# Talking-heads attention and a squared-ReLU FFN on one core: spread scores for 30 chunks of the first batch, checked row sums, FFN units in four 64x64 tiles, and a new order of TensorE's units

## The chip, the cores and the metric

The kernel runs on one core of a Trainium2 chip. The metric is the device time of one execution in microseconds (us). Inputs and output lie in HBM as float32; inside the kernel all matmul operands are bf16 and all sums are float32 in PSUM.

## What is computed

There are 8 batches, 12 heads, 448 positions and a head dimension of 64. The scores of the 12 heads are mixed by a 12x12 matrix before the softmax (pre-mixing), the probabilities by another after it (post-mixing). The result, 3584 tokens of 768 features, goes through an FFN of width 2048 with squared ReLU.

```python
scores = scale * np.matmul(q, k.transpose(0, 1, 3, 2))      # 8 x 12 x 448 x 448
scores = np.einsum('bhij,hg->bgij', scores, w_pre)
scores = scores - np.max(scores, axis=-1, keepdims=True)
attn = np.exp(scores)
attn = attn / (np.sum(attn, axis=-1, keepdims=True) + 1e-09)
attn = np.einsum('bhij,hg->bgij', attn, w_post)
attn_out = np.matmul(attn, v)
x = attn_out.transpose(0, 2, 1, 3).reshape(B * S, H * D)    # 3584 x 768
out = np.square(np.maximum(x @ w_in, 0.0)) @ w_out          # 768 -> 2048 -> 768
```

Softmax does not change when a constant is subtracted from all scores of a row. The kernel before uses this and never computes the maximum: it takes exp of the mixed scores as they are.

## The kernel before

**Chunks.** The 448 query positions of a batch are cut into chunks of 10 (`CH`), 45 chunks per batch, the last of 8 handled as two of 4. A chunk of 10 positions by 12 heads fills 120 of 128 partitions: one row per (position, head), 448 keys along the free axis. Chunks go in pairs.

**The usual way of a chunk** (batches 1 to 7, and chunks 22 to 44 of batch 0). `emit_QK` (L891) computes scores of a query tile of 128 positions, two heads at a time (64 rows each, the array in two row tiles) or, for a rest of 64 positions, four at a time in four 64x64 tiles; the result is copied from PSUM to the tile `stage` by ScalarE or VectorE (L460 or L461, in the helper `copy`). A DMA of SyncE's queue (`emit_rel`, L947) then moves a chunk's rows from `stage` into the ring `dring`, so that (position, head) lies on partitions. `emit_pre` (L969) mixes the heads of a pair of chunks with four matmuls in four 64x64 tiles; `after_pre` (L989) takes exp on ScalarE with the row sum beside it (L994), the reciprocal on VectorE (L1008), and multiplies it into the post-mixing weights on GpSimd (L1015). `emit_post` (L1029) does the post-mixing with 16 short matmuls (L1047), whose results are copied to `a2t`.

**The direct way** (chunks 0 to 21 of batch 0). To start without a DMA, VectorE multiplies the transposed queries of batch 0 with the pre-mixing weights (`emit_scale`, L821, 36 instructions at L834), into space that `w_out_sb` and `h2t` do not need yet. `emit_direct` (L846) then gets mixed scores straight from six matmuls of the whole 128x128 array per chunk (L856):

```python
for p in ps_:                                                      # six pairs of heads
    r_ = eng.matmul(ps[:, g.banks[0], 0:S], qs[:, p, y:y + 2, :].rearrange("p i g -> p (i g)"),
                    qkt[:, 0, p, 1, :], start=(p == 0), stop=(...))
```

**AV and FFN.** `emit_AV` (L1090) multiplies a half batch (220 or 228 positions) with V in 64x64 tiles (L1104) and in two column tiles (L1125), and the result is copied to `xt`. `emit_F1` (L1163) is the first FFN layer: a unit gives two of the sixteen 128-blocks of the hidden layer. In batches 0 and 1 (`NFULL = 2`) it uses the whole array (L1173, called "full"), later two row tiles of 64x128 (L1194, "row"). `after_F1` (L1219) does the ReLU on ScalarE or VectorE into one of three buffers `h1t`, and VectorE squares it into `h2t` (L1235). `emit_F2` (L1296) is the second layer, in row tiles (L1316); its result goes to `osb` and by GpSimd's DMAs to the output. The last two tiles use the whole array and SyncE's and ScalarE's queues (`emit_last`, L1256; L1265, L1288).

**What sets the order.** Every piece of work is a task with an engine, a mode of tiling and dependencies. `_Plan` commits the tasks one by one: the other engines' by readiness, TensorE's units in the order of the string `ORDER` (L29), whose digits name ten streams (0 transposes, 1 QK, 2 pre-mixing, 3 post-mixing, 4 AV, 5 direct scores, 6 and 7 first FFN layer, 8 and 9 second). A task marked FLEX goes to ScalarE or VectorE, as the plan's costs have it. Each engine then runs its list in that order, and waits are semaphores. PSUM has eight banks; a unit takes one or two and holds them until they are copied out. A unit whose mode differs from that of the unit before it is a change of tiling; there are 244 in TensorE's list, between modes full (128x128), row (64x128), cols (128x64) and quad (64x64).

At the start TensorE runs some matmuls on constants ("warm", L583) while it waits for the first loads.

Of the kernel before, what the change touches and what calls it, by code (L numbers as in the profile page):

```python
# [23 lines left out]
EVENTS = {"tr": 0.12, "qk": 0.72, "di": 0.2, "po": 0.61, "pr": 1.1, "av": 0.43, "o0": 0.43}  # L24
# [3 lines left out]
INF = float("inf")  # L28
ORDER = (  # L29
    "0001155500055555555555555555513155511155555331555533355551135555552005113555555330023324"  # L30
    "2443310041316261116722326772267633227713367333761142441114223667227631167713226671136713"
    "3277620029333912293921812283383338240024442002661118111833381118132672226773136713376224"
    "2444227761136711166333620027622813822383383337771422444200116667733002277622181183118133"
    "8339122922933912291191139333924244422163613731711631622007227363216372227610016733720208"
    "1383338113822291911393119224244422383138311831384222444223621617311716331620027337226336"
    "2127372001636217337220093191119131922833831181138242444222919313933392242444228318331811"
    "1833622267317216362200733733622167200173622367131720029319131931192228181338113822283833"
    "1842244442444238161336220073373362226761171716337610026733724244412812283382020839111911"
    "3913392291192229319138333811382424442283611673317622673137163167122762226733791229339213"
    "98338242444228338338222868633837226773667733677646444876766776678766776879989999899888"  # L40
# [12 lines left out]
class _Task:  # L53
# [3 lines left out]
                 "done", "bias", "sync", "group", "instrs", "issued", "later", "two")  # L57

    def __init__(self, name, engine, fn, deps, after, cost, prio, sem, seminc, mode, dma,
# [18 lines left out]
        self.sync = ()  # L78
        self.done = self.issued = False
# [9 lines left out]
class _Group:  # L89
# [4 lines left out]
    def __init__(self, n):  # L94
        self.n = n
        self.banks = None
        self.readers = [[] for _ in range(n)]


class _Plan:  # L100
# [44 lines left out]
    def _commit(self, t, e, start):  # L145
# [5 lines left out]
        self.free[e] = start + held  # L151
        t.end = start + lat
# [93 lines left out]
    def _commit_pe(self, t, start):  # L246
        if t.mode != self.mode:
            self.mode = t.mode
        g = t.group
        if g is not None and g.banks is None:  # L250
            _, got = self.find(g.n, self.free[PE])
            g.banks = sorted(got)
            for i, readers in zip(g.banks, g.readers):
# [3 lines left out]
                self.bank_users[i] = readers  # L257
                self.age += 1
                self.bank_age[i] = self.age
# [8 lines left out]
    def next_unit(self, order, at):  # L268
        if at >= len(order):
            return None  # L270
        t = self.streams[int(order[at])][0]
        if t.nwait:
            return None
        est = max(self.free[PE], t.avail)
        if t.group is not None and t.group.banks is None:
            est = max(est, self.find(t.group.n, self.free[PE])[0])
        if t.mode != self.mode:
            est = max(est, self.free[PE] + MODE_SWITCH)
        return (est, t) if est < INF else None

    def run(self, order=""):
        self.start()
        at = 0
        while True:
# [15 lines left out]
            if f is not None and (best is None or f[0] <= best[0]):  # L300
# [3 lines left out]
                self.streams[int(order[at])].pop(0)  # L304
                at += 1
                self._commit_pe(f[1], f[0])
# [12 lines left out]
def bass_talking_heads_attention__then__ffn_squared_relu_kernel(  # L319
# [18 lines left out]
    ND = 22  # L338
    NDW = 16
    DH = 4  # L340
# [23 lines left out]
    with ExitStack() as es:  # L364
# [6 lines left out]
        NDS = 16  # L371
        NPS = 10
# [4 lines left out]
        NFULL = 2  # L377
# [8 lines left out]
        wq = sb("wq", [128, NP, H, H5], DT.bfloat16)  # L386
        wall = sb("wall", [128, NP, 2, H], DT.float32)
        mask2 = sb("mask2", [128, H5], DT.float32)
        wrep2 = sb("wrep2", [128, H], DT.float32)
        wk1 = sb("wk1", [128, 64], DT.bfloat16)  # L390
        wk2b = sb("wk2b", [128, H, H5], DT.bfloat16)
        wk2s = sb("wk2s", [128, NPS, PR], DT.bfloat16)
        rowsum = sb("rowsum", [128, NPS, 1], DT.float32)
# [17 lines left out]
        zrow = sb("zrow", [128, S], DT.bfloat16)  # L411
# [4 lines left out]

        def Sm(name):
            return _Sem(nc.alloc_semaphore(name), name)
# [5 lines left out]
        sem_z = Sm("dz")  # L424
        sem_qk = [[Sm("dqk%d_%d" % (i, x)) for x in range(2)] for i in range(3)]
        sem_v = Sm("dv")
        sem_wq = Sm("dwq")
# [3 lines left out]
        sem_last = Sm("olast")  # L431
        sem_out = [Sm("oslot%d" % i) for i in range(NOS)]

        plan = _Plan(NB)

        def c_pe(t):
            return {PE: (t, t + 190.0)}

        def c_ev(cols):
            return {ACT: (cols / 1.2 + 65.0, cols / 1.2 + 175.0),  # L440
                    DVE: (cols / 0.96 + 72.0, cols / 0.96 + 160.0)}

        def add(name, engine, fn, deps, cost, prio, mode=None, group=None, instrs=0):
            return plan.add(name, engine, fn, deps, cost, prio, "ctr", 1, mode, group=group,
                            instrs=instrs)

        events = {}

        def unit(s, name, fn, deps, ns, mode, group, mms):
            kind = name[:2]  # L450
            was = events.get(kind, 0.0)
            events[kind] = was + EVENTS.get(kind, 0.5)
            n = 2 * mms + int(events[kind]) - int(was)
            t = add(name, PE, fn, deps, c_pe(ns), 0, mode, group, n)
            s.append(t)
            return t

        def copy(eng, en, o, i_):
            if en == ACT:
                return eng.activation(o, i_, AF.Copy)  # L460
# [1050 lines left out]
```

## Time and profile before

| | |
|---|---|
| time, median of 3 runs | 526.3 us (523.89 to 526.61) |
| time of the profiled execution | 521.03 us |
| its span (first to last instruction) | 519.0 us |
| TensorE clock granted | 1.000 |

The profile is one execution. A span row gives an engine's busy time; a slice row has one digit for each of 40 slices of about 13 us, the busy share in tenths. TensorE's matmuls are pipelined, so the duration of one matmul overlaps with the next: what a unit costs is read from the start of one group in the timeline to the start of the next, not from its duration. PE is TensorE's matmuls, PEld its weight loads, DVE VectorE, ACT ScalarE, POOL GpSimd, SP SyncE.

### The profile page before, as it was taken

The page shows a single profiled execution, that of the slowest core. Times are in us where ns is not written, and L with a number is a line of the kernel's source. Part 1 is how long each engine was busy: PE and PEld are TensorE (multiplying, and loading weights), DVE is VectorE, ACT ScalarE, POOL GpSimd, SP SyncE. Part 2 cuts the span into 40 slices and gives each one's busy share as a digit, 9 for nine tenths or more (in the row PEclk, how much of TensorE's full clock was granted, in tenths as well). Part 3 has the DMA queues.
Part 4 walks back from the last instruction along what each step waited for, and adds up shares of the span by engine and source line. Part 5 has one row for each costly group of instructions (what it writes and reads, how often), then busy time and mean ns, then how long its engine had stood idle before and what let it go on. Part 6 is the DMA issues. An engine that isn't in the chain of part 4 may idle for free.

```text
span 519.0 us, 23210 instructions
## 1 busy us (share of the span) xinstructions
PE 505.7 (97%) x9632; PEld 320.0 (62%) x9632; DVE 397.4 (77%) x999; ACT 418.5 (81%) x1206; POOL 204.1 (39%) x404
## 2 busy tenths in 40 slices
PE   7998999999999999999999999999999999999997
PEld 3455767577776564666555665566556565568874
DVE  6966989889889677978897778975897668865430
ACT  3688999889988889898998889988878886887310
POOL 9913445425651455134632357124722332332000
PEclk9999999999999999999999999999999999999999
DMA  8999999746984689647984679537965557632003
GB/s 156 198 217 170 187 192 194 168 109 146 167 177 106 144 162 183 134 87 164 175 163 91 141 165 182 128 72 156 192 103 111 125 131 139 123 87 66 4 23 99
DMA packets 82560, 71.85 MB, mean 138 GB/s; under 512 B 13434, under 2 KB 79946, under 8 KB 82458
## 3 DMA queue, kind: packets, MB, share of 16 engines
q0 software_dynamic: 36944, 32.81, 38.8%
q1 hardware_dynamic: 45226, 37.38, 30.1%
q8 instruction: 77, 1.26, 1.0%
q10 hardware_dynamic: 288, 0.20, 0.1%
q14 instruction: 25, 0.20, 0.1%
HBM read 45.70 MB, written 11.01 MB: 109 GB/s over the span
## 4 chain that ended last, share of the span: by engine, by line
PE 87%; DMA 5%; DVE 4%; ACT 2%; issue 1%; SPq 1%; POOL 0%; POOLq 0%; DVEq 0%
PE ps L1316 26%; PE ps L1194 18%; PE ps L1047 7%; PE ps L977 7%; PE ps L1173 6%; PE ps L1125 6%; PE ps L908 6%; PE ps L856 5%; DMA dring<-stage 3%; PE ps L1265 2%; DVE stage L461 2%; PE ps L759 1%; DMA qraw<-in_q_dram 1%; PE ps L1104 1%; ACT pring L994 1%
## 5 line engine op out<-in xcount | busy, mean ns | idle before, releaser
L994 ACT ACTIVATE pring<-ps 128x448 bf16<-128x448 f32 x360 | 191.1, 555 | 16.3 <-PE ps L977 10.3
L1316 PE MATMUL ps<-w_out_sb,h2t 64*128 64x384 bf16 x1664 | 152.0, 323 | 0.6 <-issue 0.6
L1015 POOL TENSOR_TENSOR wk2s<-wk2b,rinv 128x120 bf16<-128x120 bf16 (+1 forms) x179 | 69.8, 392 | 189.8 <-DVE rinv L1008 188.6
L461 DVE CAST a2t<-ps 128x480 bf16<-128x480 f32 (+1 forms) x192 | 117.3, 640 | 14.7 <-PE ps L1047 13.2
L1194 PE MATMUL ps<-xt,w_in_sb 64*128 64x448 bf16 (+2 forms) x1344 | 121.9, 323 | 0.2
L461 DVE CAST stage<-ps 128x448 bf16<-128x448 f32 (+1 forms) x174 | 104.5, 617 | 15.4 <-PE ps L908 11.5
L460 ACT ACTIVATE stage<-ps 128x448 bf16<-128x448 f32 (+1 forms) x186 | 96.6, 551 | 23.0 <-PE ps L908 21.1
L1316 PEld LDWEIGHTS ps<-w_out_sb,h2t 64*128 64x128 bf16 x1664 | 77.1, 94 | 52.4 <-issue 3.6
L460 ACT ACTIVATE a2t<-ps 128x480 bf16<-128x480 f32 (+1 forms) x176 | 92.8, 574 | 13.6 <-PE ps L1047 13.2
L1194 PEld LDWEIGHTS ps<-xt,w_in_sb 64*128 64x128 bf16 x1344 | 62.2, 94 | 40.4 <-PE ps L977 2.2
L1348 POOL DMA_DIRECT2D out_dram<-osb x59 | 37.1, 634 | 111.3 <-ACT pring L994 42.2
L994 ACT ACTIVATION_READ_ACCUMULATOR pring<-ps 128x1 f32 x360 | 79.0, 219 | 0.0
L1047 PEld LDWEIGHTS ps<-wk2s,pring 60*128 60x128 bf16 x2880 | 56.1, 93 | 21.4 <-issue 3.1
L1047 PE MATMUL ps<-wk2s,pring 60*128 60x60 bf16 x2880 | 61.1, 187 | 1.0 <-issue 0.3
L1226 DVE TENSOR_SCALAR h1t<-ps 128x448 bf16<-128x448 f32 (+2 forms) x102 | 49.0, 488 | 16.5 <-PE ps L1194 14.1
L1008 DVE RECIPROCAL rinv<-rowsum 128x2 f32<-128x2 f32 (+1 forms) x184 | 29.1, 158 | 35.9 <-ACT pring L994 35.0
L977 PE MATMUL ps<-dring,wk 60*64 60x448 bf16 (+1 forms) x676 | 54.5, 362 | 1.5 <-DVE stage L461 0.6
L1235 DVE TENSOR_TENSOR h2t<-h1t 128x448 bf16<-128x448 bf16 (+2 forms) x176 | 52.6, 332 | 0.5 <-ACT h1t L1225 0.2
L908 PE MATMUL ps<-qkt 64*128 64x448 bf16 (+1 forms) x360 | 49.8, 354 | 1.4 <-issue 1.4
L1225 ACT ACTIVATE h1t<-ps 128x448 bf16<-128x448 f32 (+2 forms) x74 | 32.9, 456 | 19.7 <-PE ps L1194 18.0
L1173 PE MATMUL ps<-xt,w_in_sb 128*128 128x220 bf16 (+1 forms) x384 | 41.7, 260 | 0.1
L1173 PEld LDWEIGHTS ps<-xt,w_in_sb 128*128 128x128 bf16 x384 | 34.6, 98 | 5.7 <-DVE h1t L1226 0.9
(59 smaller groups left out, 419.3 us busy)
## 6 DMA issues: line engine op xcount, KB each, us to landing
dring<-stage SPq DMA_DIRECT2D x309, 105.0 KB
out_dram<-osb POOLq DMA_DIRECT2D x45, 192.0 KB, 4.0
qraw<-in_q_dram POOLq DMA_DIRECT2D x42, 112.0 KB, 5.5
kraw<-in_k_dram POOLq DMA_DIRECT2D x42, 112.0 KB, 5.3
w_in_sb<-in_moe_w_in_dram POOLq DMA_DIRECT2D x8, 384.0 KB, 12.7
w_out_sb<-in_moe_w_out_dram POOLq DMA_DIRECT2D x8, 384.0 KB, 8.7
vraw<-in_v_dram POOLq DMA_DIRECT2D x21, 128.0 KB, 5.1
vraw<-in_v_dram POOLq DMA_DIRECT2D x21, 96.0 KB, 5.3
```

Source lines behind the costliest of these rows:

```text
L460: return eng.activation(o, i_, AF.Copy)
L461: return eng.tensor_copy(o, i_)
L908: r_ = eng.matmul(ps[y * w:(y + 1) * w, g.banks[x], 0:S], qkt[r0:r0 + 64, pb, p + y, 0, i0:i0 + w], qkt[r0:r0 + 64, pb, p + y, 1, :], star ...
L977: r_ = eng.matmul(ps[64 * y:64 * y + 64, gr.banks[x], 0:S], wk1[64 * x:64 * x + 64 - R0 * x, :], dring[64 * x:64 * x + 64 - R0 * x, (g0 + ...
L994: return eng.activation(pring[:, pr, 0:S], ps[:, gr.banks[x], 0:S], AF.Exp, accum_out=rowsum[:, pr, :])
L1015: return eng.tensor_tensor(wk2s[:, p0:p0 + n, :], i0.to_broadcast([128, n, PR]), rinv[:, p0:p0 + n, :].to_broadcast([128, n, PR]), ALU.mult)
L1047: r_ = eng.matmul(ps[:, gr.banks[x], o0:o0 + PR], pring[64 * x:64 * x + PR, pr + y, j0:j0 + 2 * PJ], wk2s[64 * x:64 * x + PR, pr + y, :], ...
L1173: r_ = eng.matmul(ps[:, g.banks[0], 0:n], w_in_sb[:, ft, t * 128:(t + 1) * 128], xt[:, ft, c0:c1], start=(ft == 0), stop=(ft == NFT - 1))
L1194: r_ = eng.matmul(ps[:, g.banks[x], 0:n], w_in_sb[64 * y:64 * y + 64, ft, t * 128:(t + 1) * 128], xt[64 * y:64 * y + 64, ft, c0:c1], start ...
L1226: return eng.tensor_scalar(h1t[:, s, 0:n], ps[:, g.banks[x], 0:n], 0.0, None, op0=ALU.max)
L1235: return eng.tensor_tensor(h2t[:, t16, o0:o0 + n], h1t[:, s, 0:n], h1t[:, s, 0:n], ALU.mult)
L1316: r_ = eng.matmul(ps[:, g.banks[hh], 0:FH], h2t[64 * y:64 * y + 64, t16, col:col + 128], w_out_sb[64 * y:64 * y + 64, t16, hh * FH:(hh + 1 ...
```

## The change

Line numbers with "after" are of the changed kernel.

1. **Spread scores.** The direct way goes. For chunks 0 to 29 of batch 0 (`ND` from 22 to 30), `emit_spread` (after L889) copies the queries of each pair of heads unscaled into a zeroed layout `qz` in `h2t`, in 12 copies of 64 partitions x 300 elements (FLEX). `emit_spr` (after L902) computes unmixed scores of a chunk with eight matmuls in four column tiles of 128x32, four at a time; a FLEX copy brings the 128x448 result from PSUM to `dring`; the pre-mixing of these chunks is one matmul of the whole array per chunk, with weights `wkf` that a new small DMA (`wrepf`, four transfers on SyncE's queue) and two VectorE operations prepare. The 36 multiplications, the weights for them, the DMA that zeroed rows of `dring`, and the moves of chunks 22 to 29 through `stage` go. Two fills of 1920 float32 elements per partition (one on VectorE, one on ScalarE) zero `qz` at the start. The loads of `w_out` no longer wait for the direct scores.

```diff
-                    r_ = eng.matmul(ps[:, g.banks[0], 0:S],
-                                    qs[:, p, y:y + 2, :].rearrange("p i g -> p (i g)"),
-                                    qkt[:, 0, p, 1, :],
+                    for n, col, p in todo:
+                        r_ = eng.matmul(ps[32 * col:32 * col + 32, g.banks[0], 0:S],
+                                        qz[:, c, 2 * col + n, :], qkt[:, 0, p, 1, :],
+                                        start=(n == 0), stop=(n == 1))
...
+                def fn_sev(eng, en):
+                    return copy(eng, en, dring[:, c % NDS, :], ps[:, g.banks[0], 0:S])
...
+                    if g0 < ND:
+                        for g in gs:
+                            r_ = eng.matmul(ps[:, gr.banks[g - g0], 0:S],
+                                            wkf[:, :, :].rearrange("p i g -> p (i g)"),
+                                            dring[:, g % NDS, :], start=True, stop=True)
+                        return r_
```

2. **Tiling by unit.** Units of both FFN layers, QK units of 128 positions and pre-mixings can run in one of two or three tilings (`_Flex`, after L107), and the order string says which: a digit is the tiling as before, a letter another one. In quad an FFN unit has four matmuls of 64x64 where the row tiling has two of 64x128. In full, a unit's two halves take one bank each, as they come.

```diff
                         for y in range(2):
                             x = ph ^ y
                             t = t16 + x
+                            for z in range(0, 128, w):
                                 r_ = eng.matmul(
-                                ps[:, g.banks[x], 0:n],
-                                w_in_sb[64 * y:64 * y + 64, ft, t * 128:(t + 1) * 128],
+                                    ps[z:z + w, g.banks[x], 0:n],
+                                    w_in_sb[64 * y:64 * y + 64, ft,
+                                            t * 128 + z:t * 128 + z + w],
                                     xt[64 * y:64 * y + 64, ft, c0:c1],
```

3. **A new order** of TensorE's units (`ORDER`, and with it the lists of all engines). There are 228 changes of tiling in it.

4. **Checked row sums.** All 368 row sums are kept, and after the last exp three VectorE operations test whether each lies between 1e-30 and 1e30; a DMA on SyncE's queue brings the 128 results onto one partition, and VectorE reduces them to one flag. The whole program is built a second time with the row maximum subtracted, and stands in the instruction streams as the taken side of a branch: each engine loads the flag into a register and branches. With sums in range, each engine jumps over this second program to the rest of its list. TensorE branches at its end; ScalarE in front of its last 25 tasks, VectorE of its last 11 (squares), GpSimd and SyncE in front of the last output DMAs.

```diff
+            emit_tasks(eng_name, eng, tasks[:k], fast_waits)
+            eng.wait_ge(t_flag.sem.handle, t_flag.semval)
+            fine = eng.value_load(flag[0:1, 0:1])
+            with eng.If(fine == 0):
+                emit_tasks(eng_name, eng, tasks[k:], fast_waits)
...
+                emit_tasks(eng_name, eng, slow[eng_name], slow_waits)
+            if k < len(tasks):
+                with eng.Else():
+                    emit_tasks(eng_name, eng, tasks[k:], fast_waits)
```

TensorE's list before the branch has 10417 matmuls, against 9632 before. By unit, first layer of the FFN: 62 full, 74 row and 40 quad (before: 64 full, 112 row); second layer: 16 full, 84 row and 12 quad (before: 8 full, 104 row). Of 169 pre-mixings in the usual way, 159 are quad and 10 row (before: 173 quad).

More of the change, by code (lines that the diff above doesn't have):

```diff
@@ L431, in bass_talking_heads_attention__then__ffn_squared_relu_kernel @@
         sem_last = Sm("olast")
+        sem_good = Sm("dgood")
         sem_out = [Sm("oslot%d" % i) for i in range(NOS)]
[L434 to L460, printed above, removed]
-            return eng.tensor_copy(o, i_)
@@ L1455, in emit_engine @@
[L1455 to L1456 removed]
+                               NFT * (n / 2.4 + 4.3), "row", g, 2 * NFT, f,
+                               [("full", NFT * (n / 2.4 + 2.5), NFT),
+                                 ("quad", NFT * (n / 2.4 + QFIX), 4 * NFT)], ph)
+                    t_h.sync = [before] if ph else []
+                    before = t_h
+                f1_done(b, parts, t16, t_h)
+                for x in range(2):
+                    t_r = after_F1(b, parts, t16 + x, t_h, c0, n, g, x)
+                    if x == 0:
+                        f.early.append(t_r)
```

1842 lines of the change are left out of this document (997 added, 845 removed).

## The prediction

> **What bounds the kernel now.** I read the page's busy times and slices first, then the chain.
>
> ```profile
> span 519.0 us, 23210 instructions
> PE 505.7 (97%) x9632; PEld 320.0 (62%) x9632; DVE 397.4 (77%) x999; ACT 418.5 (81%) x1206; POOL 204.1 (39%) x404
> PE   7998999999999999999999999999999999999997
> PE 87%; DMA 5%; DVE 4%; ACT 2%; issue 1%; SPq 1%; POOL 0%; POOLq 0%; DVEq 0%
> q8 instruction: 77, 1.26, 1.0%
> ```
>
> TensorE is busy in every slice and carries 87% of the chain: the kernel gets faster by what TensorE is spared, as long as the others keep up. Whether they do is read by stage (columns: window and its length, then busy us of each engine).
>
> ```profile
> 13.00:52.00 39.00, 36.94 (x623) 20.40 (x617) 29.87 (x84) 30.92 (x89) 17.89 (x32) 1.00 1.14 195
> 52.00:104.00 52.00, 50.84 (x942) 35.59 (x938) 47.17 (x133) 48.33 (x148) 25.46 (x50) 1.00 0.96 185
> 104.00:519.00 415.00, 408.57 (x7904) 258.76 (x7898) 311.54 (x753) 334.72 (x963) 148.94 (x297) 1.00 0.62 127
> ```
>
> From 13 to 52 us (direct scores) VectorE has 9.1 us free and ScalarE 8.1; from 52 to 104 they are 91% and 93% busy, nearly as full as TensorE; later 75% and 81%. So there is a tight place, just behind the part that is rewritten.
>
> A busy PE says nothing of its price per unit. That is read from starts in the timeline:
>
> ```profile
> 250.36 1.30 PE L1194 MATMUL ps<-xt,w_in_sb 64*128 64x448 bf16 x12
> 251.49 0.61 PE L1047 MATMUL ps<-wk2s,pring 60*128 60x60 bf16 x32
> ...
> 252.13 1.30 PE L1194 MATMUL ps<-xt,w_in_sb 64*128 64x448 bf16 x12
> 253.36 0.38 PE L977 MATMUL ps<-dring,wk 64*64 64x448 bf16 x4
> ...
> 254.21 0.38 PE L977 MATMUL ps<-dring,wk 64*64 64x448 bf16 x4
> 254.52 1.31 PE L1194 MATMUL ps<-xt,w_in_sb 64*128 64x448 bf16 x12
> ...
> 261.32 0.36 PE L908 MATMUL ps<-qkt 64*64 64x448 bf16 x4
> 261.51 0.38 PE L977 MATMUL ps<-dring,wk 64*64 64x448 bf16 x4
> ```
>
> An FFN unit followed by another row unit takes 251.49 - 250.36 = 1.13 us, six rounds of 0.189; followed by a quad unit 253.36 - 252.13 = 1.23. A change into quad costs 0.10. Back, a pre-mixing takes 0.31 until the row unit starts (254.52 - 254.21), against 0.19 from quad to quad (261.51 - 261.32): 0.12. I use 0.10 per change of tiling.
>
> **The change, part by part.** First TensorE.
>
> ```profile
> 13.23 7.55 PE L856 MATMUL ps<-qkt,w_out_sb 128*128 128x448 bf16 x39
> 20.71 0.36 PE L908 MATMUL ps<-qkt 64*128 64x448 bf16 x2
> ...
> 47.01 1.32 PE L1125 MATMUL ps<-a2t,vraw 128*64 128x220 bf16 x24
> 48.27 0.62 PE L1047 MATMUL ps<-wk2s,pring 60*128 60x60 bf16 x32
> ```
>
> (20.71 - 13.23 - 0.10) / 39 = 0.189 us per direct matmul. *Direct scores go*: 22 chunks x 6 x 0.189 = -24.9. *Spread scores come*: eight matmuls in four column tiles are two rounds; 24 chunks do them in one unit, 6 chunks in three units of one round, so 24 x 2 + 6 x 3 = 66 rounds. The trace has no 128x32 tile; but its 128x64 tiles (L1125) run two at a time at full rate, 24 in 1.26 - 0.10, so twelve rounds of 0.097 for 220 columns; 66 x 0.189 = +12.5. *Their pre-mixing*: 30 matmuls of the whole array, +5.7. Four pre-mixings in quad (chunks 22 to 29) go, -0.8; ten others take two rounds instead of one, in row tiling, +1.9. One warm matmul less, -0.2. Sum -5.8. *Changes of tiling*: 244 to 228, 16 x 0.10 = -1.6. TensorE together: **-7.4 us**, of which 5.3 fall before the second batch's AV, at 104 us of the old trace (counted with the same prices in both lists).
>
> *FFN units in quad* (40 of 176 first-layer units, 12 second-layer; 40 x 6 + 12 x 8 = 336 rounds): I cost a round like one in row tiling. Before has quad rounds, never 24 in a row; the nearest is two pre-mixings and a transpose:
>
> ```profile
> 195.81 0.57 PE L977 MATMUL ps<-dring,wk 64*64 64x448 bf16 x8
> 196.21 0.39 PE L759 MATMUL ps<-ident,qraw 64*64 64x64 bf16 x28
> 196.43 0.43 PE L759 MATMUL ps<-ident,kraw 64*64 64x64 bf16 x28
> ```
>
> Two rounds in 0.40: 0.02 above 2 x 0.19, once per entry, and contained in the price of a change. A transpose puts 28 loads and 28 matmuls into 0.22 us, so neither issue nor loading limits four tiles. I take 0; if every round paid what the first does (0.024: the 0.40 are 0.213 and 0.189, read finer), it would be +8.1. Nothing excludes a gain, but no row suggests one.
>
> *ScalarE and VectorE*, in the first 50 us:
>
> ```profile
> L834 DVE TENSOR_TENSOR w_out_sb<-qkt,wq 128x480 bf16<-128x480 bf16 x24 | 9.6, 445 | 0.1
> L834 DVE TENSOR_TENSOR h2t<-qkt,wq 128x480 bf16<-128x480 bf16 x6 | 2.6, 444 | 0.0
> L834 DVE TENSOR_TENSOR h2t<-qkt,wq 128x240 bf16<-128x240 bf16 x6 | 1.5, 293 | 0.0
> L547 DVE TENSOR_SCALAR wq<-wall 64x180 bf16<-64x180 f32 x4 | 1.2, 330 | 0.6 <-DMA wall<-in_w_pre_dram 0.6
> L816 ACT ACTIVATE w_out_sb<-wk 128x768 bf16<-128x768 bf16 x1 | 0.8, 842 | 0.0
> L460 ACT ACTIVATE stage<-ps 128x448 bf16<-128x448 f32 x149 | 76.9, 555 | 19.4 <-PE ps L908 18.0 <-issue 1.1
> L461 DVE CAST stage<-ps 128x448 bf16<-128x448 f32 x127 | 75.7, 615 | 11.1 <-PE ps L908 10.0 <-PE ps L1047 0.3
> L461 DVE COPY qkt<-ps 128x448 bf16<-128x448 bf16 x11 | 3.9, 380 | 0.7 <-PE ps L755 0.7
> L519 DVE MEMSET zrow<- 4x224 uint32 x1 | 0.2, 245 | 0.1
> ```
>
> Gone: 13.7 us of multiplications, 1.2 of weights, about 1.2 of fills. Added: 30 copies from PSUM, half on each engine, 15 x 0.555 + 15 x 0.615 = 17.6; twelve query copies of 300 elements, about 0.3 each, 3.6; two zero fills of 1920 elements (224 take 0.245, 768 on ScalarE 0.84), about 2.0 each, 4.0. Net +9 of busy time for the two. The fills fall into the wait for the first loads, so some 5 remain. At 13 to 52 us there were 9.1 + 8.1 = 17.2 free; less 5, and less 5.3 on each engine because TensorE would be through sooner, 1.6 remain, with chunks now passing two more hand-overs each (score copy, pre-mixing) before exp. They cannot be used to the last: I let **+2.0** of the 5.3 be lost, between 0 and 5.3.
>
> ```profile
> 4.06 0.63 DVE L461 CAST qraw<-xt 128x896 bf16<-128x896 f32 x1 [1.15 <-DMA xt<-in_q_dram]
> 52.96 0.74 PE L1173 MATMUL ps<-xt,w_in_sb 128*128 128x220 bf16 x6
> ```
>
> *Start*: VectorE casts the first queries when they land, after a wait of 1.15 us; its fill takes 2.0, less the 0.2 of the old one, so some 0.3 to 0.7 are late, of which transposes that wait for later loads hide part: +0.3 (0 to 1). The second row is the first FFN unit, to which I come back. The new weight DMA has until the first pre-mixing.
>
> *Instruction supply*: 785 more matmuls, each with its load, are 1570 instructions. The 77 instruction packets stand for 19,264 of them plus waits, so about six packets more.
>
> ```profile
> PE ps L908 <- issue: 1.4, 1, 1.4
> PE ps L1125 <- issue: 0.9, 1, 0.9
> ```
>
> These are the two largest waits of TensorE for nothing but its own instructions, 2.3 us or 0.03 per packet: +0.3 with some more in small ones (0 to 2.4, six gaps of 0.4).
>
> *Checks and branch*: three VectorE operations on 368 values, about 0.45 each, lie in the last stage, where it is 75% busy. VectorE then waits for the flag's DMA, with three squares in front of it; behind it are the squares of the last first-layer units, and behind these ScalarE's ReLUs (three buffers) and so PSUM banks. Then ScalarE and VectorE jump.
>
> ```profile
> 492.92 3.67 PE L1194 MATMUL ps<-xt,w_in_sb 64*128 64x228 bf16 x72
> 496.43 1.46 PE L1316 MATMUL ps<-w_out_sb,h2t 64*128 64x384 bf16 x16
> 497.73 0.75 PE L1194 MATMUL ps<-xt,w_in_sb 64*128 64x228 bf16 x12
> ```
>
> Six first-layer units of the last half batch take 3.51, 0.585 each, and half a second-layer unit 1.30. TensorE's own jump, and SyncE's and GpSimd's, come when nothing waits behind them. Let a jump hold its engine for J. While ScalarE jumps, TensorE has six free banks, so ScalarE's jump alone stops nothing. By my estimate from the groups of ReLUs and squares, VectorE reaches its jump 2.0 after ScalarE is back (four ReLUs and an output copy; not before 4.2, when TensorE has the units done), and needs 0.7 after it for three squares. TensorE wants these for a second-layer unit after ten first-layer units and one of 1.30, 7.1 us from the start. TensorE waits max(J + 2.0, 4.2) + J + 0.7 - 7.1: nothing up to J = 2.1. The nearest row is the longest gap above, 1.4 (a fetch that came too late); the upper row is a whole small transfer.
>
> ```profile
> out_dram<-osb SPq DMA_DIRECT2D x6, 96.0 KB, 2.2
> ```
>
> I take J = 2.4, the upper row and a little for the request: max(4.4, 4.2) + 2.4 + 0.7 - 7.1 = 0.4, and as much again for the flag's wait: **+0.8** (0 to 3.5).
>
> [...]
>
> Sum: -7.4 + 2.0 + 0.3 + 0.3 + 0.8 = -4.0. The profiled execution took 521.03, so 517.0; the median of the runs is 526.3, 1.0101 times that execution, so **522.3 us**, 0.8% less. A measurement of this kernel can tell about 0.5%, 2.6 us, from no change.
>
> **The rivals.** *Full gain*: ScalarE and VectorE keep up in the first 104 us. For it: at 52 to 104 us TensorE was 98% busy with them at 93%. -7.4 + 1.4 = -6.0 gives 515.0, or 520.2 as a median (518.8 if nothing else costs either).
>
> *The copies bind the first stage*: all that TensorE saves by 104 us is given back as waiting. For it: VectorE and ScalarE at 91 and 93% right behind. -7.4 + 5.3 + 1.4 = -0.7: 525.6, the same.
>
> *Quad rounds are slower*: each of 336 rounds pays 0.024, for each tile must be loaded before the next round. For it: the first of two quad rounds is 0.02 longer. Against it: from quad to quad it takes 0.19. -4.0 + 8.1 = +4.1: 530.4, slower. It decides from 0.012 a round (no gain), and is slower by more than 0.5% from 0.020.
>
> [...]
>
> *The jumps are dear*: with J of 3.5 TensorE waits 2.6, with J of 6 it waits 7.6, place and formula as above: -4.0 - 0.4 + 2.6 = -1.8 to +3.2, so 524.5 to 529.5. [...]
>
> **How the numbers follow.** Forecast 0.40 (520.5 to 524.5; three quarters of it beyond 0.5%), full gain 0.22, copies bind 0.14 (a fifth of it slower), quad rounds 0.10, jumps 0.14 (half the same, half slower). Faster: 0.30 + 0.22 = 0.52. Same: 0.10 + 0.11 + 0.07 = 0.28. Slower: 0.03 + 0.10 + 0.07 = 0.20. The range leaves out the slow quad rounds and the outer end of the full gain: 518 to 529.
>
> **What would show it.** In the changed kernel: first-layer quad units 1.13 to 1.16 us apart (1.28 is the rival); a direct-score stage whose end, the start of the first FFN unit (52.96 before), lies 2 to 4 us earlier, with VectorE or ScalarE over 90% busy and TensorE with idle time there; from there to the end about the same number of us, 2 or 3 less; a gap of 1.5 to 3 us on ScalarE and VectorE in the last 35 us that TensorE hardly follows. Wrong it would be if TensorE's idle time rose by over 7 us in all, or if a change of tiling from 128x32 tiles cost far more than 0.10.

## The result and the profile after

The changed kernel takes 535.0 us (median of 20 runs, 525.6 to 554.0), the kernel before 525.1 (20 runs, 521.8 to 529.5). The ratio is 1.0108, 95% interval 1.0069 to 1.0146: **slower by 1.1%**, where 0.8% faster was forecast. The ratio is taken from the runs within 1.5% of each kernel's shortest, 8 of the 20 of the changed kernel (by the medians of all runs it is 1.019), and the profiled execution (540.79 us, granted clock 0.983) is a long one, so its sums overstate the loss, and ratios, not profiles, say below what an edit is worth.

The page of the changed kernel: span, TensorE's busy time, its slices and granted clock, the chain by engine, SyncE's DMA queue and the instruction queues.

```profile
span 538.9 us, 24764 instructions
PE 508.7 (94%) x10417; PEld 332.5 (62%) x10417; DVE 394.2 (73%) x977; ACT 433.3 (80%) x1240; POOL 204.3 (38%) x404
PE   8999999998989997999899969999999989999896
PEclk9999999998999998999999979999999999999999
q1 hardware_dynamic: 44250, 36.39, 30.2%
q8 instruction: 85, 1.39, 1.0%
q14 instruction: 34, 0.28, 0.1%
PE 77%; DMA 8%; ACT 6%; DVE 3%; POOL 3%; issue 2%; SPq 0%; POOLq 0%; DVEq 0%
```

TensorE is busy for 3 us more in a span 20 us longer: it idles where it did not before, in slices that read 7, 6 and 8, with dents in the clock beside them. DMA has gone from 5% to 8% of the chain. Busy time by stage (window, its length, then busy us of TensorE, its loads, VectorE, ScalarE, GpSimd; clock):

```profile
13.00:52.00 39.00, 37.59 (x782) 18.86 (x782) 35.62 (x89) 37.64 (x112) 19.97 (x36) 1.00 1.14 188
52.00:104.00 52.00, 50.74 (x1173) 37.12 (x1170) 45.83 (x124) 47.99 (x149) 26.14 (x52) 1.00 0.94 184
104.00:539.00 435.00, 409.47 (x8269) 270.97 (x8267) 302.66 (x731) 339.86 (x969) 146.36 (x291) 0.98 0.62 120
```

The first two stages are as good as before. The loss lies behind 104 us, where ScalarE and VectorE have room: TensorE has 25.5 us there without work, against 6.4 before. What it waits for is read from the tile `stage`, through which all scores of the usual way go. First the kernel before, then the changed one; the first row is SyncE's moves from `stage` to `dring` (count, then ns of one issue: least, median, most; first and last start), the second the idle time of ScalarE and VectorE in front of a copy into `stage` that ended when such a move landed (us, times).

```profile
L954 SPq DMA_DIRECT2D dring<-stage x367: 673/823/2832, 25.0 to 464.9; - x184
...
  DMA dring<-stage: 0.7, 1
```

```profile
L1029 SPq DMA_DIRECT2D dring<-stage x359: 682/913/3343, 30.4 to 480.6; - x180
...
  DMA dring<-stage: 22.6, 9
```

0.7 us of such waits have become 22.6. Why TensorE follows is seen in the timeline of the changed kernel at the longest one:

```profile
305.96 14.18 SPq L1029 DMA_DIRECT2D dring<-stage  x13
...
310.20 0.57 ACT L524 ACTIVATE a2t<-ps 128x480 bf16<-128x480 f32 x1 [0.39 <-PE ps L1154]
313.30 0.62 DVE L525 CAST stage<-ps 128x448 bf16<-128x448 f32 x1 [5.26 <-DMA dring<-stage]
...
314.58 0.55 PE L984 MATMUL ps<-qkt 64*128 64x448 bf16 x2 [4.42 <-DVE stage L525]
...
315.57 0.57 ACT L524 ACTIVATE a2t<-ps 128x480 bf16<-128x480 f32 x1 [4.80 <-PE ps L1154]
```

`stage` has two halves. The copies of a tile of 128 positions may start when all moves out of its half, two tiles back, have landed. VectorE runs its list in order, so it stands 5.26 us in front of the copy, whose PSUM banks stay taken; TensorE's next QK unit waits 4.42 us for a bank, and ScalarE then 4.80 us for TensorE.

To weigh this I took each unit's start to the next unit's start, less the price of its kind and 0.095 us per change of tiling, as TensorE's **stall**: 24.5 us in all before, 50.2 after. The last matmul ends 18.4 us later: 25.7 more stall, 7.4 less unit work. The forecast's saving is there, and a loss more than three times as large that it does not name.

### The profile page after: what moved, and what is told of

Same layout as the page of the kernel before. It is cut to its first block, busy times and chain, and to the rows that moved or that the text cites. A ratio compares the mean times of both kernels' runs of the same rounds, so it can differ in the third digit from the quotient of the medians.

```text
span 538.9 us, 24764 instructions
## 1 busy us (share of the span) xinstructions
PE 508.7 (94%) x10417; PEld 332.5 (62%) x10417; DVE 394.2 (73%) x977; ACT 433.3 (80%) x1240; POOL 204.3 (38%) x404
## 3 DMA queue, kind: packets, MB, share of 16 engines
q1 hardware_dynamic: 44250, 36.39, 30.2%
## 4 chain that ended last, share of the span: by engine, by line
PE 77%; DMA 8%; ACT 6%; DVE 3%; POOL 3%; issue 2%; SPq 0%; POOLq 0%; DVEq 0%
PE ps L1430 23%; PE ps L1291 18%; PE ps L1154 7%; DMA dring<-stage 7%; PE ps L1283 6%; PE ps L1068 6%; PE ps L1232 5%; PE ps L984 5%; ACT pring L1093 3%; PE ps L1422 2%; PE ps L1370 2%; PE ps L836 2%; DVE stage L525 2%; DMA kraw<-in_k_dram 1%; POOL vraw L737 1%
## 5 line engine op out<-in xcount | busy, mean ns | idle before, releaser
L1430 PE MATMUL ps<-w_out_sb,h2t 64*128 64x384 bf16 (+1 forms) x1728 | 142.9, 325 | 0.2
L525 DVE CAST stage<-ps 128x448 bf16<-128x448 f32 (+1 forms) x185 | 111.0, 617 | 30.6 <-DMA dring<-stage 16.5
L1291 PE MATMUL ps<-xt,w_in_sb 64*64 64x448 bf16 (+4 forms) x1848 | 128.5, 328 | 0.8 <-DVE stage L525 0.6
L524 ACT ACTIVATE stage<-ps 128x448 bf16<-128x448 f32 (+1 forms) x175 | 91.0, 552 | 22.3 <-PE ps L984 14.9
L1430 PEld LDWEIGHTS ps<-w_out_sb,h2t 64*128 64x128 bf16 (+1 forms) x1728 | 74.7, 97 | 45.5 <-issue 3.2
L1291 PEld LDWEIGHTS ps<-xt,w_in_sb 64*64 64x64 bf16 (+1 forms) x1848 | 71.5, 101 | 34.4 <-ACT pring L1093 1.7
L1068 PE MATMUL ps<-dring,wk 64*64 64x448 bf16 (+1 forms) x620 | 54.7, 362 | 7.2 <-DVE stage L525 4.5
L1328 ACT ACTIVATE h1t<-ps 128x448 bf16<-128x448 f32 (+2 forms) x93 | 40.0, 450 | 20.7 <-PE ps L1283 12.7
L1115 DVE RECIPROCAL rinv<-rowsum 128x2 f32<-128x2 f32 (+1 forms) x184 | 28.9, 158 | 25.5 <-ACT pring L1093 24.6
L1329 DVE TENSOR_SCALAR h1t<-ps 128x448 bf16<-128x448 f32 (+2 forms) x83 | 41.5, 506 | 6.7 <-PE ps L1291 3.5
L1283 PE MATMUL ps<-xt,w_in_sb 128*128 128x220 bf16 (+2 forms) x372 | 43.9, 272 | 0.3 <-ACT osb L524 0.3
## 6 DMA issues: line engine op xcount, KB each, us to landing
w_in_sb<-in_moe_w_in_dram POOLq DMA_DIRECT2D x8, 384.0 KB, 10.6
```

The costliest lines, as they stand in the source:

```text
L525: return eng.tensor_copy(o, i_)
L1068: r_ = eng.matmul(ps[64 * y:64 * y + 64, gr.banks[x], 0:S], wk1[64 * x:64 * x + 64 - R0 * x, 64:128], dring[64 * x:64 * x + 64 - R0 * x, ( ...
L1283: r_ = eng.matmul(ps[:, g.banks[ph], 0:n], w_in_sb[:, ft, t * 128:(t + 1) * 128], xt[:, ft, c0:c1], start=(ft == 0), stop=(ft == NFT - 1))
L1291: r_ = eng.matmul(ps[z:z + w, g.banks[x], 0:n], w_in_sb[64 * y:64 * y + 64, ft, t * 128 + z:t * 128 + z + w], xt[64 * y:64 * y + 64, ft, c ...
L1329: return eng.tensor_scalar(h1t[:, s, 0:n], ps[:, g.banks[x], 0:n], 0.0, None, op0=ALU.max)
L1430: r_ = eng.matmul(ps[z:z + w, g.banks[hh], 0:FH], h2t[64 * y:64 * y + 64, t16, col + z:col + z + w], w_out_sb[64 * y:64 * y + 64, t16, hh ...
```

## The experiments

Three theories at first. *One*: the new order asks for score copies before the moves have landed. *Two*: the guard (checks, flag, jumps, second program). *Three*: quad units or the instruction supply. A fourth came when the first fell.

**A third buffer, its control, the guard, the planner's landing time.** A third half of `stage` needs 10.5 KB per partition, of which narrowing the second FFN weight frees 10.0; the control has the narrow weight alone. With it a kernel computes the second half of the output from the wrong columns of the weight (64 to 448) and loads less of it. The lists of all engines are those of the changed kernel. Of this edit and those below the main lines are shown, with notes added behind `#`.

```diff
-        w_out_sb = sb("w_out_sb", [128, NFFT, F], DT.bfloat16)
+        w_out_sb = sb("w_out_sb", [128, NFFT, 448], DT.bfloat16)
-        stage = sb("stage", [IT, 2, H, S], DT.bfloat16)       # third half only
+        stage = sb("stage", [IT, 3, H, S], DT.bfloat16)
-                sl = n % 2
+                sl = n % 3                                    # and waits on rel_of[n - 3]
```

> Control for the next run: the changed kernel with the second FFN weight kept as 448 columns of 768 (the second half of the output is computed from columns 64 to 448, and 1.3 MB less are loaded in the first stage). All theories: as the changed kernel, 1.011 of the kernel before (1.005 to 1.017); the engines' idle time before score copies that ends with a landing move stays near 22.6 us.

> As the control, with a third buffer for the scores and every list of every engine unchanged, so that a score copy waits for the moves of three tiles back and not two. Theory 1 (the new order puts score copies before the moves have landed): the idle time before copies that ends with a landing move falls from 22.6 to under 3 us, TensorE's stalls between units from 50 to under 33 us, no stretch at half clock, 10 to 18 us under the control (0.98 to 0.99 of before). Theory 2 (the guard's checks and jumps) and theory 3 (four-tile FFN rounds or instruction supply are slower): within 2 us of the control.

Measured: control 1.0182 (1.0123 to 1.0241), median 535.6; third half 0.9909 (0.9834 to 0.9985), median of all its 12 runs 527.6. The interval is wide, so I take the difference of the medians, 8 us. The row of waits for landing moves is gone, TensorE's stalls fall from 51.6 to 33.5 us, and no stretch at half clock is left (granted clock 0.999). So the waits for a half of `stage` are the loss. The row of the moves at `stage`, though, stays as in the changed kernel, 931 ns in the median:

```profile
L1031 SPq DMA_DIRECT2D dring<-stage x359: 682/931/3936, 29.8 to 463.6; - x180
```

```diff
-            if not guard:                      # the checks, the flag
+            if False:
-        slow, slow_waits, _ = program(True)    # and the jump with it
```

> The changed kernel without the check of the row sums, the flag, the jump and the second program; the lists are otherwise the same. Theory 1: 1 to 5 us under the changed kernel (1.002 to 1.009 of before), all of it in the last 35 us. Theory 2: 10 us or more under it (0.985 to 0.992), because the code of the second program, the load of the flag and the jump are gone. Theory 3: no more than theory 1.

1.0138 (1.0076 to 1.0200), waits 25.1 us in 11 places: theory two is out; the guard costs nothing that shows against the changed kernel.

```diff
-DMA_END = {"move": 2800.0, "load": 2300.0}
+DMA_END = {"move": 5500.0, "load": 2300.0}
```

> The changed kernel with the planner's landing time of a move raised from 2.8 to 5.5 us (the measured median from issue to landing is 4.9 us), which changes the lists of ScalarE and VectorE but not TensorE's order: score copies stand later in them, behind work that is ready. Theory 1: the blocked engines go on with other work, idle time before copies that ends with a landing move falls under 12 us, and the time falls to 0.995 to 1.005 of before. Theories 2 and 3: 1.011, unchanged.

1.0232 (1.0171 to 1.0294): the waits of copies fall to 7.8 us as theory one says, but the time does not: stalls are 49.0 us. The waiting is still there, in many small groups of TensorE's waits; the largest, 11.0 us in front of the weight loads of pre-mixings (6.8 in the changed kernel), ends with nothing that the profile shows.

**What holds the halves.** A move may also stand on SyncE until its slot of the 16 in `dring` is free. `ring26` has 26 slots (and the narrow weight), `ring18` has 18 and the full weight, both with unchanged lists; `third_no_guard` joins two edits from above; `qk_later` shifts QK units in the order string.

```diff
-        NDS = 16
+        NDS = 26            # ring18: 18; each move waits on pre_at(g - NDS)
```

> As the control, with two staging halves but 26 chunk slots in the ring that the moves write instead of 16, every list of every engine unchanged: a move no longer waits for the pre-mixing of 16 chunks back but of 26. Theory 1a (a move stands on SP until a ring slot is free, so that the halves are held by TensorE's own later work): waits of copies for landing moves fall from 22 to under 6 us and the time to that of the third half, 0.985 to 0.995 of before. Theory 1b (the moves' issue and landing alone hold the halves): over 15 us of these waits stay and the time is 1.010 to 1.018.

> The whole changed kernel, guard and all, with 18 ring slots instead of 16 (the warm-up's tile shares the output buffer's memory) and every list unchanged. Theory 1a: two slots let each move go about one pre-mixed pair (2 to 3 us) earlier, copies' waits fall from 22 to under 12 us, time 0.995 to 1.005 of before. Theory 1b: unchanged, 1.010 to 1.018.

> Third staging buffer and no row-sum check, flag, jump or second program. If waits for the halves and the guard are all that stands between the forecast and the result: 2 to 4 us under the third half with the guard, 0.982 to 0.988 of before, TensorE's stalls between units 30 us or less. If instruction supply or the four-tile rounds cost as well: no gain over the third half, stalls stay at 33 us.

> The changed kernel with every QK unit from the first batch's seventh on put six places later in TensorE's written order (about 3 us), two halves and 16 slots. Theory 1 in the form that the order asks for copies too early: copies' waits for landing moves fall under 12 us and the time to 1.000 to 1.008 of before. In the form that the staging cycle is itself the limit (about 27 of 30 us of each tile's turn are taken): the waits move from the copies to the pre-mixings that need the later moves, and the time stays at 1.010 to 1.025.

26 slots: 1.0239 (1.0192 to 1.0286), waits 23.1 us; 18 slots: 1.0227 (1.0159 to 1.0295), 14.3 us. Theory 1a falls: slots are not what the moves wait for. Third half without guard: 1.0011 (0.9969 to 1.0054), stalls 33.3 us, no clear gain over the third half with it (medians 525.8 and 527.6). By what was expected that speaks for a cost of instruction supply or of quad rounds besides; both are priced in the next section from the changed kernel, 1.9 us for the one and nothing for the other, and what else lies in 33.3 us of stalls against 24.5 before these runs do not divide. QK later: 1.0999 (1.0914 to 1.1083), far above the 1.025 that was the most expected. Some 10 us of that are 105 more changes of tiling, which the shift brought with it; the waits of copies are gone, and now the pre-mixings wait, which need the moves (waits of TensorE in `qk_later`: us, times, longest):

```profile
PE ps L1068 <- DMA dring<-stage: 10.5, 9, 2.7
```

These waits are a part of the loss; where the rest comes from was not taken apart. Earlier the copies wait, later the pre-mixings: the chain through `stage` has little room in either direction. By the issue and landing records of the moves, a tile's turn on its half takes 9.8 us of copies, 0.7 to the first issue, 12.7 of issues and 3.6 to the last landing, 26.9 of the 29.2 us between two tiles of one half in the kernel before. It has 8 to 14 moves, and SyncE issues them one behind the other: 12.2 us of issue time on average in the 14.6 us between tiles. That is 83%. Over the same stretch of the kernel before, from 51 to 465 us, ScalarE is busy for 364.53 of 414 us, 88%, and VectorE for 338.01, 82%: the queue has no more room than VectorE.

**The order.** If the new order is at fault, the old one behind the first stage must cure it. The order string can be cut where both kernels have the same units left (the edit in short; in the kernel the string itself is replaced).

```diff
-ORDER = after[:969]
+ORDER = after[:204] + before[201:]     # old_rest; 608 and 605 in old_rest_608
```

> The changed kernel's first 204 units (spread scores, about 97 us), then the order and the tilings of the kernel before for all the rest (260 changes of tiling); guard and second program as in the changed kernel. Theory 1 (the new order after the first stage asks for score copies too early): the first stage's gain of 5 us is kept, waits of copies for landing moves are under 2 us, and the time is 0.988 to 0.996 of before. Theory 2 (guard) or 3 (code of four-tile units in the first stage, instruction supply): 1.005 to 1.018.

> The same with the cut at unit 608 (about 300 us): the new order up to there, the old one behind it. Theory 1: the waits of copies before 300 us stay (about half of the changed kernel's 22.6 us), those behind it go; time between the two, 1.000 to 1.010 of before.

> The changed kernel's order of units, with each unit after the first stage in the tiling that it has in the kernel before (no four-tile FFN unit, QK in two row tiles): 379 changes of tiling instead of 228, so 151 x 0.095 = 14.3 us more on TensorE by the spacing of units. Theory 3 (four-tile rounds are slower than others): the rounds give back more than 5 us and the time rises by under 9 us over the changed kernel. Theory 1: the rounds cost the same; TensorE's units grow by 13 to 16 us, and a part of it, 4 to 8 us, is won back because the slower TensorE lets moves land before copies; time 1.025 to 1.038 of before.

Old order from unit 204 on: **1.0236** (1.0135 to 1.0336). TensorE's and GpSimd's lists behind the cut are those of the kernel before, the others' too but for a few pieces of work that trade places and the guard's own; still the waits at `stage` are there:

```profile
L1029 SPq DMA_DIRECT2D dring<-stage x359: 666/917/3095, 29.9 to 482.1; - x180
...
  DMA dring<-stage: 19.2, 6
```

So theory one falls: it is not the order. The cut at 608 gave 1.0132 (1.0060 to 1.0205), above the 1.000 to 1.010 that was expected, and 12.0 us of waits, of which 6.6 lie behind the cut, where they should have gone. In `old_forms` (1.0310, 1.0250 to 1.0370) 151 more changes are 14.3 us by the spacing; the time rises by 2.0% over the changed kernel, 10.6 us, and stalls are 35.3. Theory three had under 9; by the medians of all runs, though, the rise is only 0.7%, so this run alone does not rule it out. The price of a quad unit does, which the next section reads as 1.14 us. That waits and stalls are smaller here fits a slower TensorE that lets the moves catch up.

**The addresses.** What do all these kernels share, if not the order, the guard or the slots? In each the median issue of a move lies at 887 to 955 ns, before at 823. Added up, 359 issues take 370.1 us in the changed kernel, 1031 ns each, and 367 took 360.5 before, 982 ns each. A slower move leaves no room in a chain that is 83% full. And the change does touch what the moves read, though no line of it says so: the small tensors that it adds and removes lie ahead of the large ones in SBUF. They end at byte 19,968 before, 78 x 256, and at 21,344 after, 333 x 64 and 32. The tensors between are 87,552 = 342 x 256 bytes, so `stage` started at a multiple of 256 and now starts 96 bytes past one, which is 32 past a multiple of 64 (the narrow weight and the third half leave that as it is). An unused pad, `align`, stands ahead of the large tensors in both kernels; three runs change its length alone. They put `stage` 128 bytes past a multiple of 256 (pad of 96), at a multiple of 256 (pad of 224), and, in the kernel before, 224 past one, again 32 past a multiple of 64.

```diff
-        sb("align", [128, 64], DT.uint8)
+        sb("align", [128, 96], DT.uint8)    # pad96; 224 in pad224; 32 in the kernel before
```

> The changed kernel with its unused pad of 64 bytes made 96, so that all large tensors start at a multiple of 64 bytes again (128 for the staging buffer, which was at 32 past a multiple of 64). Theory 4 (the shift by 32 bytes makes each move's issue longer): mean issue back to 970 to 1000 ns, waits of copies for landing moves from 22.6 to under 6 us, time 0.985 to 0.995 of before. Theory 1 (the order, or the chain whatever the addresses): 1.010 to 1.022, issue 1030 to 1050 ns.

> The same with a pad of 224 bytes: multiples of 256, as in the kernel before. Theory 4: as the pad of 96 or a little better, 0.985 to 0.995. Theory 1: 1.010 to 1.022.

> The kernel before with its pad of 64 bytes made 32, so that all large tensors start 32 bytes past a multiple of 64. Theory 4: mean issue rises from 982 to 1030 to 1055 ns, copies begin to wait for moves (over 8 us where 0.7 us was), time 1.010 to 1.030 of before. Theory 1: unchanged, 0.997 to 1.003.

Pad of 96: **0.9960** (0.9911 to 1.0010). Pad of 224: **0.9982** (0.9945 to 1.0020). The kernel before with the shift: **1.0283** (1.0235 to 1.0330). The page of `before_off32`, span and SyncE's queue (packets, MB, share of 16 engines' span), and behind it its moves and waits at `stage`:

```profile
span 535.0 us, 23210 instructions
q1 hardware_dynamic: 45226, 37.38, 31.4%
```

```profile
L954 SPq DMA_DIRECT2D dring<-stage x367: 672/923/2757, 24.9 to 480.8; - x184
...
  DMA dring<-stage: 23.8, 13
```

The same two views of `pad96`, and the second of `pad224`:

```profile
span 526.5 us, 24764 instructions
q1 hardware_dynamic: 44250, 36.39, 28.6%
```

```profile
L1029 SPq DMA_DIRECT2D dring<-stage x359: 682/815/2988, 30.3 to 466.7; - x180
...
  DMA dring<-stage: 6.8, 4
```

```profile
L1029 SPq DMA_DIRECT2D dring<-stage x359: 677/813/2727, 30.6 to 468.8; - x180
...
  DMA dring<-stage: 10.9, 5
```

The medians fall from 913 to 815 and 813 ns, and rise from 823 to 923 with the shift. With the pads the ratios lie a little above the 0.985 to 0.995 that was expected, and the waits above the 6 us. The queue's row says the same of the packets: 16 x 0.302 x 538.9 / 44250 = 58.8 ns each in the changed kernel, 16 x 0.286 x 526.5 / 44250 = 54.4 with the pad, 59.4 in the kernel before with the shift. Nothing but a pad differs: theory four is shown, in both directions.

**Which end of the move.** 32 unused bytes ahead of a tensor and 32 behind it put that one alone back.

```diff
+        sb("pad_s", [128, 32], DT.uint8)
         stage = sb("stage", [IT, 2, H, S], DT.bfloat16)
+        sb("pad_d", [128, 32], DT.uint8)
         dring = sb("dring", [128, NDS, S], DT.bfloat16)      # only_source; only_dest: around dring
```

> The changed kernel with 32 unused bytes ahead of the staging buffer and 32 behind it: of all large tensors only the staging buffer, the source of the moves, starts at a multiple of 64 bytes. If the source decides: mean issue 960 to 1000 ns and 0.994 to 1.002 of before. If the destination decides: 1030 to 1055 ns and 1.010 to 1.020. If both count: about 1000 to 1020 ns and 1.003 to 1.012.

> The same with only the ring of chunk slots, the destination of the moves, at a multiple of 64 bytes. If the destination decides: mean issue 960 to 1000 ns and 0.994 to 1.002 of before. If the source decides: 1030 to 1055 ns and 1.010 to 1.020. If both count, or if other tensors' addresses do: in between.

> The first 204 units of the changed kernel, the old order and tilings behind them, and the pad of 96 bytes. If what the changed kernel still lacks with the pad is due to the new order: the first stage's 4 to 5 us stay to the end, 0.985 to 0.993 of before. If the order does not matter: 0.994 to 1.000, as with the pad alone (32 more changes of tiling, 3 us).

> The control of the narrow second weight with a third staging buffer and the pad of 96 bytes. If the two staging halves still cost with the pad: 3 to 6 us under the changed kernel with the pad, 0.984 to 0.991 of before. If the shift was all that the third half cured: 0.993 to 0.999.

Source alone: 0.9983 (0.9940 to 1.0026). Destination alone: 1.0236 (1.0185 to 1.0288). Moves and waits at `stage` of the one, then of the other:

```profile
L1031 SPq DMA_DIRECT2D dring<-stage x359: 666/811/2678, 30.2 to 470.3; - x180
...
  DMA dring<-stage: 9.6, 5
```

```profile
L1031 SPq DMA_DIRECT2D dring<-stage x359: 666/927/2884, 29.8 to 472.7; - x180
...
  DMA dring<-stage: 18.9, 11
```

The source decides alone: with it alone put back the median issue is 811 ns, with the ring alone 927, and at the starts tried here, those of the ring and of the other large tensors make no difference. A row here is 896 bytes, 3.5 x 256. From a multiple of 128, rows begin in turn 0 and 128 past a multiple of 256. From 96 past a multiple of 256, as `stage` lay, they begin in turn 96 and 224 past; from 224 past, as in the kernel before with the shift, the same two in turn. With rows that begin so, a packet took 8% longer (58.8 against 54.4 ns); a start 128 past a multiple of 256 costs what a multiple of 256 does (815 and 813 ns). Why a row that begins at 96 or 224 past costs more no run here shows.

Old order with the pad: 0.9994 (0.9959 to 1.0029), no wait for a landing move any more. Third half with the pad: 0.9956 (0.9924 to 0.9987), median 522.8 against 525.4. It has the lowest median of all, but needs the memory of half a weight. Of the kernels with the whole weight none is faster than the kernel before by more than the measurement can tell; the pads come closest, with 0.9960 and 0.9982.

| run | ratio to before | median issue, ns | waits of copies, us |
|---|---|---|---|
| changed kernel | 1.0108 | 913 | 22.6 |
| small_w / third_half | 1.0182 / 0.9909 | 937 / 931 | 25.9 / 0 |
| no_guard / third_no_guard | 1.0138 / 1.0011 | 909 / 955 | 25.1 / 0 |
| ring26 / ring18 | 1.0239 / 1.0227 | 933 / 947 | 23.1 / 14.3 |
| late_moves / qk_later | 1.0232 / 1.0999 | 937 / 928 | 7.8 / 0 |
| old_rest / old_rest_608 / old_forms | 1.0236 / 1.0132 / 1.0310 | 917 / 887 / 923 | 19.2 / 12.0 / 10.7 |
| before_off32 / only_dest | 1.0283 / 1.0236 | 923 / 927 | 23.8 / 18.9 |
| pad96 / pad224 / only_source | 0.9960 / 0.9982 / 0.9983 | 815 / 813 / 811 | 6.8 / 10.9 / 9.6 |
| old_rest_pad96 / third_pad96 | 0.9994 / 0.9956 | 817 / 830 | 0 / 0 |

## Why the prediction was wrong, step by step

Rows of the changed kernel's timeline for the steps below: the first cast of queries, the first FFN unit, a first-layer quad unit up to the next unit, and the jump.

```profile
4.11 0.56 DVE L525 CAST qraw<-xt 128x896 bf16<-128x896 f32 x1
...
47.65 1.30 PE L1283 MATMUL ps<-xt,w_in_sb 128*128 128x220 bf16 x12
...
453.25 1.31 PE L1291 MATMUL ps<-xt,w_in_sb 64*64 64x448 bf16 x24
454.39 0.55 PE L1068 MATMUL ps<-dring,wk 64*64 64x448 bf16 x8
...
511.84 0.65 DVE L1338 TENSOR_TENSOR h2t<-h1t 128x228 bf16<-128x228 bf16 x3 [3.34 <-issue]
...
512.55 1.47 PE L1422 MATMUL ps<-w_out_sb,h2t 128*128 128x384 bf16 x8 [1.72 <-DVE h2t L1338]
```

- **TensorE's units, -7.4**: right. The second batch's AV starts 5.7 us earlier (98.75 against 104.48), and the end differs by the stalls less 7.4.
- **Quad rounds, 0**: right. A unit of 24 quad matmuls takes 454.39 - 453.25 = 1.14 us, against 1.13 for one of row tiling. The rival at 530.4 came near the measured time and is still wrong: its mechanism is not there.
- **ScalarE and VectorE, +2.0 in the first stage**: too high. The first FFN unit starts 5.3 us earlier, more than the 2 to 4 forecast, with ScalarE busy for 37.64 of 39 us.
- **Start, +0.3**: too high; the cast starts 0.05 us later (4.11 against 4.06).
- **Instruction supply, +0.3**: 8 more packets on q8 where six were forecast. TensorE's waits for its own instructions sum to 5.1 us in four groups of the waits; before they were 3.2. In the two traces these are ten gaps, and each ends 1.2 to 1.7 us behind the end of a packet on q8. So 1.9 us where 0.3 was taken: too low, within the bound of 2.4.
- **Checks and jump, +0.8**: the mechanism is right, J is mis-sized. The kernel before has no jump, so no trace showed J: the forecast's 2.4 was an estimate, and so were the 3.5 to 6 of the rival with dear jumps. VectorE's jump left it idle for 3.34 us; the formula then gives 5.34 + 3.34 + 0.7 - 7.1 = 2.3, and TensorE waited 1.72. (A slip that changes nothing: by that formula TensorE waits for nothing up to J = 2.2, not 2.1.)
- **What failed** is none of the terms but one set to zero without a word. For everything behind the first stage the prediction looked at TensorE, ScalarE and VectorE, took "75% and 81%" as room, and gave SyncE's queue and the two halves of `stage` no row. The two shares are averages up to 519 us; while the moves run they are 82% and 88%, and SyncE's queue is 83% taken. The page does not show it: issue instructions count for no engine's busy time, and "SPq 1%" in the chain says only that no wait ended there while it kept up. The prediction also kept the price of a move as it was. The 32 bytes made the issue of a move 5% longer in the mean (982 to 1031 ns), the room per tile went, and TensorE stalled 25.7 us more in the profiled execution; 6.9 us of that lie in stretches at half clock. "Wrong it would be if TensorE's idle time rose by over 7 us in all" is what happened.
- **Without the shift** the forecast ratio of 0.992 lies in one interval (pad of 96: 0.9911 to 1.0010) and outside two others (pad of 224: from 0.9945; source alone: from 0.9940). Waits of 6.8 and 10.9 us remain there that the old order with the pad does not have, and the third half with the pad has the lowest time: so the new order seems to lose in a chain without room a part of what it saves on TensorE. This is the smaller part; its size, by my estimate about 2 us, is no more than these runs can tell, and stays open.

## What to carry to other kernels

Add up the issues of each DMA queue before you say where there is room: a queue at 83% is a resource like an engine, though no busy row shows it. A diff that adds or removes small SBUF tensors moves all those behind them; compare their start addresses, and test a pad, before you look for reasons in the order of the work. A slower kernel whose waits sit at a buffer need not have a wrong order: undo the order first, then look at what both versions do not share.

## What the runs showed of the hardware that was not expected

The start address of these moves' source in SBUF set their price: from 32 bytes past a multiple of 64 a packet took 58.8 and 59.4 ns, from a multiple of 128 54.4, and the median issue 913 to 927 against 811 to 815 ns, while the two starts of the destination that were tried made no difference.

TensorE's clock fell to half after short waits. In the changed kernel it did so four times before the last matmul, for 3.4, 3.4, 6.8 and 3.4 us; two of them by windows (the column behind the five engines is the clock):

```profile
210.00:214.00 4.00, 3.27 (x38) 1.43 (x42) 3.29 (x7) 2.42 (x6) 1.44 (x3) 0.57 0.75 135
313.00:320.00 7.00, 5.42 (x64) 3.03 (x66) 4.16 (x8) 2.01 (x4) 1.56 (x3) 0.52 0.74 137
```

They begin in or right behind idle gaps of TensorE of 1.7, 2.7, 4.4 and 2.6 us in the timeline. The length of a gap alone does not decide: behind the one of 1.73 us that ends at 128.42 us the clock fell (0.53 from 128.4 to 132 us), at VectorE's jump TensorE had one of 1.72 us, up to 512.55 us, and it did not (1.00 from 508 to 516 us). `before_off32` has gaps of 4.6 and 2.7 us, and its granted clock of 0.997 over 535.0 us leaves room for one drop of 3.4 us. What else decides no run here shows.
